# Local and global attention feeding a gated MLP on one core: a second block of two token tiles, and eight more steps turned on TensorE

## Chip, core and metric

The kernel runs on one core of a Trainium2 chip. The metric is the device time of one execution in microseconds (us). Engines are named as in the profile: PE is TensorE's matmul, PEld its weight load, DVE is VectorE, ACT is ScalarE, POOL is GpSimd, SP is SyncE, which here only issues DMAs. L580 is line 580 of the kernel.

## What is computed

For 8 batches and 8 heads of 64, 512 local and 32 global tokens: a local query sees the 32 global keys and the local keys no more than 32 positions away; a global query sees all keys. The result (4352 tokens of 512) goes through a two-layer MLP with 2048 hidden features.

```python
s_g = scale * np.matmul(q_g, k_all.transpose(0, 1, 3, 2))
out_g = np.matmul(sm(s_g), v_all)
s_ll = np.where(mask, scale * np.matmul(q_l, k_l.transpose(0, 1, 3, 2)), -1000000000.0)
s_lg = scale * np.matmul(q_l, k_g.transpose(0, 1, 3, 2))
out_l = np.matmul(sm(np.concatenate([s_lg, s_ll], axis=-1)), np.concatenate([v_g, v_l], axis=2))
x = out of attention, heads side by side
h = x @ w_in
return (h * (1.0 / (1.0 + np.exp(-h))) @ w_out).astype(np.float32)
```

## The kernel before

**Tokens and blocks.** The 4352 tokens are 34 tiles of 128: 32 local ones (batch and quarter of its 512 positions) and two of global tokens, tile 16 and tile 33. `SIZES` groups the tiles into 12 blocks: ten of three tiles and two of two at the end. For each block the MLP runs over 16 slices f of the hidden features. `first_layer` (L580) makes h for the block's tokens with 12 matmuls of 384 columns (256 in a block of two): each product is split into xh·wh, xl·wh, xh·wl. ACT takes a tanh (L586), DVE multiplies (L587), ACT rounds to gh (L589), DVE takes the remainder gl (L590). `second_layer` (L602 to L604) adds gh·wh, gh·wl, gl·wh into a PSUM bank per tile, three matmuls of 512 columns for each tile. On PE the second layer of slice f stands behind the first layer of slice f+1.

**Attention steps.** A local tile's attention is four steps k, one for each pair of heads, so steps 4t to 4t+3 belong to local tile t (of the first 16; k counts from 0, so the title's words "13 to 20" are k = 12 to 19). A step has parts:
- `st_load` (L310, L312) and, once for a tile, `st_vload` (L322): DMAs on SP's queue; from k = 28 on `st_split` (L332 to L334) makes rounded values and remainders. Steps under 28 score in fp32 (L348), the later ones in two passes (L350, L351).
- `st_scores`: scores on PE, mask and row minimum on DVE (L355), exponentials on ACT (L359), two small operations on DVE (L361, L362), the scaling of one head on ACT (L363) and one on DVE (L364). The result is a tile of probabilities.
- The probabilities must be turned, since the next matmul contracts over keys. A step under `KF` = 12 does it in `st_turn` with four transposes on PE (L392) into a PSUM bank and one copy by ACT into the tile pt (L394). A step from `KF` on uses DRAM: `st_halves` (L374) parts the fp32 words into 16-bit halves with two POOL copies, `st_away` (L379) writes them to DRAM by DMA, `st_back` (L383) brings them back with a transposing DMA. In both cases POOL adds the columns of the global queries to pt (L401, and L404 for a batch's last tile).
- `st_out` (L425): once for a tile, all four steps' outputs on PE; ACT and DVE write the MLP's inputs xh and xl (L432, L433) and DVE adds up the global part (L439).

There are four pt tiles, so a step's pt is free again when the outputs of the tile before are done. Global queries have their own parts (`g_load` L229, `g_scores` L256 to L262, `g_soft` L276 to L281, `g_turn` L296 to L302).

**Order.** PE's order is written out by hand. Every part gets a due time in units of one step (`DUE`; for steps from `KF` on also `DMAT`), the parts are sorted by it, and `fill` advances through this list after each first layer and after each tile's second layer. While block n runs, the list is advanced from the end mark of block n's tiles to that of block n+1's:

```python
            advance(ends[n] + (ends[n + 1] - ends[n]) * min(1.0, now[1] / total / FULL))
```

So a block carries the attention steps of the next block's tiles. With the turn on PE a step's turn is due 1.6 units after its scores and the outputs 2.2; with the way through DRAM the halves are due at 0.7, the DMA away at 1.05, the DMA back at 1.65 and the outputs at 2.7.

**Weights.** While block 0 runs the 16 weight blocks still arrive: SP fetches them (L193), ACT and DVE join their 64-bit words to fp32 (L209, L211, L212), ACT rounds (L221, w_hi) and DVE takes the remainder (L222, w_lo), one block ahead of the slice that uses it. The other engines' orders come from the framework's scheduler, except that operations wrapped in `hold` keep the program's order.

## Time and profile before

| what | value |
|---|---|
| three runs | 991.98, 995.24, 998.11 us (median 995.24) |
| the profiled execution | 994.48 us, span 992.6 us |
| first L580 matmul of block 0 | 47.5 us after the span's start |
| first L580 matmul of block 1 | 150.0 us |
| first L580 matmul of the blocks of two tiles | 891.8 and 940.5 us |
| DMA queue of SP | 148.6 MB, 55.3% of 16 engines' time |
| granted TensorE clock | 0.999 of full speed |

How it is read: matmuls are pipelined and their modelled spans overlap, so the busy time of PE is more than what it needs. The weight loads, one ahead of each matmul, are the better measure of its progress. A wait is put down to the releaser that came last by the profile. In a row of a group stand the line, engine, operation, tiles, shapes and count, then the busy time and the mean ns of one, then the idle time ahead of it and what ended it. In a row of a stretch stand its limits and length, then busy us and count of PE, PEld, DVE, ACT and POOL, the granted clock, the DMA engines' share and GB/s. A row of the timeline has start and length in us first.

### The profile page before, as it was taken

The page shows a single profiled execution, that of the slowest core. Times are in us where ns is not written, and L with a number is a line of the kernel's source. Part 1 is how long each engine was busy: PE and PEld are TensorE (multiplying, and loading weights), DVE is VectorE, ACT ScalarE, POOL GpSimd, SP SyncE. Part 2 cuts the span into 40 slices and gives each one's busy share as a digit, 9 for nine tenths or more (in the row PEclk, how much of TensorE's full clock was granted, in tenths as well). Part 3 has the DMA queues.
Part 4 walks back from the last instruction along what each step waited for, and adds up shares of the span by engine and source line. Part 5 has one row for each costly group of instructions (what it writes and reads, how often), then busy time and mean ns, then how long its engine had stood idle before and what let it go on. Part 6 is the DMA issues. An engine that isn't in the chain of part 4 may idle for free.

```text
span 992.6 us, 17536 instructions
## 1 busy us (share of the span) xinstructions
PE 962.2 (97%) x5790; PEld 846.9 (85%) x5790; DVE 627.6 (63%) x1894; ACT 574.4 (58%) x1479; POOL 200.8 (20%) x413
## 2 busy tenths in 40 slices
PE   8989899999999999999999999999999999999997
PEld 6667678899898889998899989998988999889896
DVE  4889975666676667745577566766667665453322
ACT  7977764556566656644566556666556655343332
POOL 2112221222122212111222222222122221220000
PEclk9999999999999999999999999999999999999999
DMA  8699967566665666534655666566665664433000
GB/s 287 224 289 262 236 169 195 154 169 168 168 168 130 197 178 164 161 98 128 170 151 160 154 178 177 165 183 154 173 175 156 155 164 141 116 91 86 1 22 22
DMA packets 190026, 157.33 MB, mean 159 GB/s; under 512 B 128752, under 2 KB 148720, under 8 KB 189936
## 3 DMA queue, kind: packets, MB, share of 16 engines
q1 hardware_dynamic: 185712, 148.61, 55.3%
q10 hardware_dynamic: 4224, 7.60, 2.2%
q8 instruction: 46, 0.75, 0.3%
q14 instruction: 44, 0.36, 0.1%
HBM read 86.44 MB, written 39.32 MB: 127 GB/s over the span
## 4 chain that ended last, share of the span: by engine, by line
PE 72%; DMA 9%; DVE 4%; ACT 3%; issue 2%; SPq 1%; POOL 0%; ACTq 0%; DVEq 0%; POOLq 0%
PE h L580 29%; PE out L602 10%; PE out L604 10%; PE out L603 10%; PE o L425 6%; DMA raw<-in_qk_dram 5%; DMA raw_g<-in_gqk_dram 2%; PE s L350 2%; PE s L351 2%; DMA away<-halves 1%; ACT qk L332 1%; DVE w L212 1%; DVE gl L590 1%; PE gt L296 1%; DVE w_lo L222 0%
## 5 line engine op out<-in xcount | busy, mean ns | idle before, releaser
L374 POOL COPY halves<-probs 128x512 uint16<-128x512 uint16 x232 | 154.1, 686 | 529.3 <-issue 319.7
L580 PE MATMUL h<-xh,w_lo 128*128 128x384 f32 (+1 forms) x768 | 252.9, 329 | 6.8 <-DVE w_lo L222 6.7
L580 PE MATMUL h<-xh,w_hi 128*128 128x384 f32 (+1 forms) x768 | 252.6, 329 | 0.4 <-ACT w_hi L221 0.3
L580 PE MATMUL h<-xl,w_hi 128*128 128x384 f32 (+1 forms) x768 | 251.5, 327 | 0.0
L602 PE MATMUL out<-w_hi,gh 128*128 128x512 f32 x544 | 221.2, 407 | 6.2 <-ACT gh L589 6.2
L604 PE MATMUL out<-w_hi,gl 128*128 128x512 f32 x544 | 215.6, 396 | 3.6 <-DVE gl L590 3.2
L603 PE MATMUL out<-w_lo,gh 128*128 128x512 f32 x544 | 213.9, 393 | 0.0
L586 ACT ACTIVATE t<-h 128x384 f32<-128x384 f32 (+1 forms) x192 | 90.4, 471 | 176.3 <-PE h L580 162.6
L587 DVE SCALAR_TENSOR_TENSOR t<-t,h 128x384 f32<-128x384 f32 (+1 forms) x192 | 101.7, 530 | 103.5 <-ACT t L586 102.5
L580 PEld LDWEIGHTS h<-xh,w_lo 128*128 128x128 f32 x768 | 144.4, 188 | 9.7 <-DVE w_lo L222 9.7
L580 PEld LDWEIGHTS h<-xh,w_hi 128*128 128x128 f32 x768 | 144.6, 188 | 8.6 <-ACT w_hi L221 1.2
L359 ACT ACTIVATE probs<-probs,st 128x224 f32<-128x224 f32 x244 | 115.7, 475 | 61.7 <-DVE st L355 60.7
L580 PEld LDWEIGHTS h<-xl,w_hi 128*128 128x128 f32 x768 | 144.6, 188 | 6.7 <-DVE xl L433 0.2
L590 DVE TENSOR_TENSOR gl<-t,gh 128x384 fp32r<-128x384 f32 (+1 forms) x192 | 106.2, 553 | 61.5 <-PE out L604 51.3
L604 PEld LDWEIGHTS out<-w_hi,gl 128*128 128x128 f32 x544 | 102.1, 188 | 33.8 <-DVE gl L590 11.0
L589 ACT CAST gh<-t 128x384 fp32r<-128x384 f32 (+1 forms) x192 | 94.3, 491 | 58.2 <-DVE t L587 58.0
L602 PEld LDWEIGHTS out<-w_hi,gh 128*128 128x128 f32 x544 | 102.6, 189 | 28.1 <-ACT gh L589 11.6
L355 DVE CUSTOM_DVE_ANT_0 probs<-s,mask 128x224 f32<-128x224 f32 x244 | 85.7, 387 | 60.0 <-PE s L351 51.1
L603 PEld LDWEIGHTS out<-w_lo,gh 128*128 128x128 f32 x544 | 102.7, 189 | 12.7
L332 ACT CAST qk<-raw 128x704 fp32r<-128x704 f32 x100 | 77.7, 777 | 40.3 <-DMA raw<-in_qk_dram 35.2
L333 DVE TENSOR_TENSOR klo<-raw,qk 128x448 fp32r<-128x448 f32 x100 | 67.0, 670 | 44.5 <-ACT qk L332 43.0
L363 ACT ACTIVATE probs<-probs,st 128x224 f32<-128x224 f32 x122 | 58.7, 481 | 39.4 <-DVE st L362 35.0
(91 smaller groups left out, 1063.0 us busy)
## 6 DMA issues: line engine op xcount, KB each, us to landing
raw<-in_qk_dram SPq DMA_DIRECT2D x100, 352.0 KB, 3.5
away<-halves SPq DMA_DIRECT2D x116, 256.0 KB, 2.6
vraw<-in_v_dram SPq DMA_DIRECT2D x30, 512.0 KB, 5.0
raw_w<-in_wts_dram SPq DMA_DIRECT2D x24, 512.0 KB, 5.9
raw_g<-in_gqk_dram SPq DMA_DIRECT2D x32, 304.0 KB, 4.4
out_dram<-o ACTq DMA_DIRECT2D x28, 256.0 KB, 3.7
raw<-in_qk_dram SPq DMA_DIRECT2D x28, 240.0 KB, 4.1
raw_w<-in_wts_dram SPq DMA_DIRECT2D x16, 256.0 KB, 4.4
```

The lines of the kernel that those rows point to most:

```text
L332: nc.scalar.copy(out=qk, in_=raw)
L355: nc.vector.tensor_tensor_reduce(out=p[:, u, :W], in0=ss[u], in1=mask_of[c], scale=-SCALE, scalar=3.0e38, op0=ALU.add, op1=ALU.min, accum_ ...
L359: nc.scalar.activation(p[:, u, :W], p[:, u, :W], AF.Exp, bias=st[:, u : u + 1], scale=-1.0, accum_out=st[:, 2 + u : 3 + u])
L374: nc.gpsimd.tensor_copy(out=halves[:, :, u], in_=p[:, 2 * P * u : 2 * P * (u + 1)].bitcast(U16).rearrange("p (j h) -> p h j", h=2))
L580: nc.tensor.matmul(h[:, :nt], wt, x[:, c, :nt], start=(i == 0), stop=(i == 3 * NCC - 1))
L586: nc.scalar.activation(t[:, :nt], h[:, :nt], AF.Tanh, scale=0.5)
L587: nc.vector.scalar_tensor_tensor(out=t[:, :nt], in0=t[:, :nt], scalar=1.0, in1=h[:, :nt], op0=ALU.add, op1=ALU.mult)
L589: nc.scalar.copy(out=gh[:, :nt], in_=t[:, :nt])
L590: nc.vector.tensor_tensor(out=gl[:, :nt], in0=t[:, :nt], in1=gh[:, :nt].bitcast(F32), op=ALU.subtract)
L602: nc.tensor.matmul(o, gh[:, sl], wh, start=(f == 0), stop=False)
L603: nc.tensor.matmul(o, gh[:, sl], wl, start=False, stop=False)
L604: nc.tensor.matmul(o, gl[:, sl], wh, start=False, stop=(f == NF - 1))
```

## The change

Two constants:

```diff
-SIZES = (3,) * 10 + (2, 2)
+SIZES = (3, 2) + (3,) * 9 + (2,)
...
-KF = 12
+KF = 20
```

The number of blocks (12) and the numbers of blocks of three and of two stay. Block 1 has two tiles and block 10, the last but one, three. Block 0 so carries steps 12 to 19 and not 12 to 23, and block 1 carries steps 20 to 31. Steps 12 to 19 take the branch of `st_turn` that has transposes; their halves, away and back are gone, and their due times are those of `DUE`:

```python
        due = dict(DUE)
        if k >= KF:
            due.update(DMAT)
            due.update({} if pr else DMAT0)
```

**SP in block 0.** Here the queue before, for two steps (raw is a step's queries and keys, raw_w a weight block, half of it from 0 and 1):

```order
L310 DMA raw_802<-in_qk_dram 128x480
L379 DMA away_810<-halves_793 128x1024
L193 DMA raw_w_839<-in_wts_dram 128x1024
L193 DMA raw_w_841<-in_wts_dram 128x1024
L383 DMA_TRANSPOSE pt_130<-away_810 128x4x256
L310 DMA raw_873<-in_qk_dram 128x480
L379 DMA away_897<-halves_875 128x1024
L193 DMA raw_w_906<-in_wts_dram 128x1024
L193 DMA raw_w_0_908<-in_wts_dram 128x512
L193 DMA raw_w_1_909<-in_wts_dram 128x512
L383 DMA_TRANSPOSE pt_131<-away_897 128x4x256
```

And in the changed kernel, from the load that stands at the same weight block:

```order
L193 DMA raw_w_818<-in_wts_dram 128x1024
L193 DMA raw_w_820<-in_wts_dram 128x1024
L310 DMA raw_863<-in_qk_dram 128x480
L193 DMA raw_w_886<-in_wts_dram 128x1024
L193 DMA raw_w_0_888<-in_wts_dram 128x512
L193 DMA raw_w_1_889<-in_wts_dram 128x512
L193 DMA raw_w_940<-in_wts_dram 128x1024
L310 DMA raw_975<-in_qk_dram 128x480
```

The DMAs away and back are gone from between the weight fetches, and a step's load comes about once in two weight blocks.

**ACT in block 0.** Before, from the tanh of slice 10 to that of slice 11 (gh is what PE's second layer of slice 10 waits for):

```order
L586 ACTIVATE t_10_1468<-h_10_1455 128x384
L363 ACTIVATE probs_86<-probs_86,st_1422 128x224
L209 ACTIVATE w_1433<-raw_w_1230 128x512
L209 ACTIVATE w_1433<-raw_w_0_1301 128x256
L209 ACTIVATE w_1433<-raw_w_1_1302 128x256
L221 CAST w_hi_1449<-w_1361 128x512 x2
L589 CAST gh_10_1469<-t_10_1468 128x384
```

And now, from the same tanh:

```order
L586 ACTIVATE t_10_1400<-h_10_1387 128x384
L363 ACTIVATE probs_85<-probs_85,st_1350 128x224
L209 ACTIVATE w_1365<-raw_w_1129 128x512
L209 ACTIVATE w_1365<-raw_w_0_1216 128x256
L209 ACTIVATE w_1365<-raw_w_1_1217 128x256
L221 CAST w_hi_1381<-w_1298 128x512 x2
L394 COPY pt_130<-t_1412 128x4x128
L209 ACTIVATE w_1425<-raw_w_1214 128x512
L209 ACTIVATE w_1425<-raw_w_0_1310 128x256
L209 ACTIVATE w_1425<-raw_w_1_1311 128x256
L589 CAST gh_10_1401<-t_10_1400 128x384
```

The PSUM copy of a turned step and a second weight's join stand ahead of gh in this slice; in other slices gh comes first, as it did.

**PE in block 1.** Now, from the fourth scores of local tile 5 (step 23) to the outputs of that tile; left out are only rows of the two MLP layers, and the outputs' middle rows:

```order
L348 MATMUL s_1800<-raw_1703 128x224 x2
...
L256 MATMUL gs_2_0_1849<-raw_g_0_1755 64x272
L256 MATMUL gs_2_0_1852<-raw_g_0_1755 64x272
...
L348 MATMUL s_1864<-raw_1768 128x224 x2
...
L348 MATMUL s_1910<-raw_1844 128x224 x2
...
L425 MATMUL o_1946<-pt_129,vraw_1739 64x160 x2
...
L425 MATMUL o_1955<-pt_132,vraw_1739 64x128 x2
```

Between the first row and the outputs stand three second layers and three first layers of two tiles each, two further scores and one global head. In block 1 before, the same stretch had layers of three tiles.

## Prediction

> **What bounds the kernel now.** I read the page first (busy shares, then the chain that ended last), then TensorE's waits in the first block, then the busy times block by block, then VectorE's and ScalarE's rows of the blocks that the change touches. The page's first part and its chain:

> ```profile
> PE 962.2 (97%) x5790; PEld 846.9 (85%) x5790; DVE 627.6 (63%) x1894; ACT 574.4 (58%) x1479; POOL 200.8 (20%) x413
> ...
> PE 72%; DMA 9%; DVE 4%; ACT 3%; issue 2%; SPq 1%; POOL 0%; ACTq 0%; DVEq 0%; POOLq 0%
> ```

> TensorE (PE) sets the end. Its matmul spans overlap, so 97% hides waits; the weight loads (PEld) show them. Next, the busy times of four stretches (PE, PEld, DVE, ACT, POOL, granted clock, DMA share, GB/s). Their limits are the first L580 matmul of a block and that of the next: block 0, block 1, block 7, block 10 (the first of the two blocks of two tiles).

> ```profile
> 47.50:150.00 102.50, 92.09 (x499) 75.35 (x498) 88.87 (x245) 71.30 (x185) 22.90 (x39) 1.00 0.85 236
> 150.00:236.90 86.90, 85.26 (x503) 74.61 (x502) 53.35 (x164) 49.79 (x131) 19.72 (x40) 1.00 0.62 164
> 649.00:731.00 82.00, 82.00 (x502) 74.28 (x501) 54.53 (x167) 50.02 (x128) 18.34 (x37) 1.00 0.62 167
> 891.80:940.50 48.70, 48.70 (x328) 43.92 (x327) 17.26 (x46) 17.38 (x45) 2.74 (x4) 1.00 0.16 44
> ```

> In blocks 7 and 10 PE never pauses, and PEld is busy 0.906 and 0.902 of the time. I take 0.905 as the share of a PE that waits for nobody. Block 0 then needs 75.35 / 0.905 = 83.3 us and takes 102.5: 19.2 us lost. Block 1 needs 82.4 and takes 86.9: 4.5 lost. Block 0 is the only place with much to win, and in it VectorE (DVE) is busy 87% and the DMA engines 85%. Whom PE waited for there:

> ```profile
> PE h L580 <- DVE w_lo L222: 6.7, 6, 2.1
> PE o L425 <- POOL pt L401: 2.3, 2, 1.3
> PE out L602 <- ACT gh L589: 0.3, 1, 0.3
> ```

> First DVE, which joins and splits a weight block per f besides its share of the attention, then two waits at the attention outputs. Other losses are pieces of 0.1 to 0.7 us.

> **The change part by part.** Two numbers move. The second block has two token tiles, so while block 0 runs the stream must bring only tiles 3 and 4 (8 steps, not 12), and the 12 steps of tiles 5 to 7 fall into block 1, which is a tile narrower. And steps 12 to 19, exactly those of block 0 now, are turned by four transposes on PE and a PSUM copy on ScalarE (ACT), not by POOL halves, a DMA out and a transposing DMA back.

> *Matmul work.* Two blocks of two tiles there were and are, so the MoE matmuls are the same set.

> *Transposes.* PE's weight loads near 37 us, and the PSUM copy on ACT:

> ```profile
> 36.98 0.42 PEld L392 LDWEIGHTS t<-ident,probs 128*128 128x128 f32 x4 [1.03 <-ACT probs L363]
> 37.37 0.68 PEld L348 LDWEIGHTS s<-raw 128*128 128x128 f32 x4
> 38.70 0.47 PEld L425 LDWEIGHTS o<-pt,vraw 128*64 128x64 f32 x8 [0.24 <-issue]
> 39.92 0.65 PEld L256 LDWEIGHTS gs<-raw_g 128*64 128x64 f32 x4 [0.17 <-issue]
> ...
> 34.82 0.56 ACT L394 COPY pt<-t 128x512 f32<-128x512 f32 x1
> ```

> Four transposes cost 0.42 / 0.905 = 0.46 us, eight steps **3.7 us** of PE, and nothing on PE goes away for them. From below 8 x 0.42 = 3.4; from above 8 x 0.66 = 5.3, with the whole matmul span of such a group. In the same way a step's scores in fp32 (L348) cost 0.75, its outputs (L425) 0.52, a global head (L256) 0.72.

> *Block 0.* Four steps and two global heads leave it: PE needs 83.3 - 4 x (0.75 + 0.52) - 2 x 0.72 + 3.7 = 80.5 us. DVE's rows of block 0:

> ```profile
> L355 DVE CUSTOM_DVE_ANT_0 probs<-s,mask 128x224 f32<-128x224 f32 x26 | 9.2, 381 | 1.0 <-PE s L348 1.0
> L364 DVE TENSOR_SCALAR probs<-probs,st 128x224 f32<-128x224 f32 x13 | 4.4, 337 | 0.5
> L433 DVE TENSOR_TENSOR xl<-o,xh 128x256 fp32r<-128x256 f32 (+1 forms) x7 | 2.8, 394 | 0.9 <-ACT xh L432 0.9
> L276 DVE TENSOR_REDUCE gst<-pg 128x1 f32<-128x544 f32 x3 | 2.1, 712 | 1.4 <-ACT pg L257 1.4
> L362 DVE RECIPROCAL st<-st 128x2 f32<-128x2 f32 x13 | 2.1, 164 | 0.4
> L355 DVE DVE_READ_ACCUMULATOR2_ANT st<- 128x1 f32 x26 | 2.1, 80 | 0.0
> L281 DVE TENSOR_SCALAR pg<-pg,gst 128x544 f32<-128x544 f32 x2 | 1.1, 552 | 0.1
> ```

> A step is 2 x (0.381 + 0.080) + 0.337 + 2 x 0.164 = 1.59 us (L361 as L362), four 6.3. One global softmax (0.71 + 0.55 + three of some 0.15) 1.7, two L433 and their accumulations some 1.2. So 9.2 us leave DVE. More goes with the halves copies: DVE and POOL disturb each other. The first L212 below runs while POOL copies halves, the second alone:

> ```profile
> 73.09 1.09 DVE L212 SCALAR_TENSOR_TENSOR w<-w,raw_w 128x512 uint32<-128x512 uint32 x1 [0.48 <-ACT w L209]
> 75.06 0.68 DVE L212 SCALAR_TENSOR_TENSOR w<-w,raw_w 128x512 uint32<-128x512 uint32 x1
> ...
> 132.64 1.10 DVE L212 SCALAR_TENSOR_TENSOR w<-w,raw_w 128x512 uint32<-128x512 uint32 x1 [0.47 <-ACT w L209]
> ...
> 72.40 1.24 POOL L374 COPY halves<-probs 128x512 uint16<-128x512 uint16 x2 [11.81 <-DMA raw_w<-in_wts_dram]
> ```

> That is 0.41 us for a meeting. Ten L212 of block 0 meet a copy (the last at 132.64), and all but a few of the copies leave it: some nine meetings, about 3.6 us. DVE falls from 88.9 to 76 us. [...]

> At DVE's present share (0.867) 76 us is 87.7 us of block 0; by PE alone it is 80.5 and with today's loss untouched 99.7. I take **89 us**, near the DVE figure, because six of the named waits are DVE's and the two L425 waits (2.3 us) lose their cause, but a little above: ACT gets 8 x 0.57 = 4.6 us of copies, which in its new order stand ahead of gh casts that PE's second layer waits for. Loss 8.5 instead of 19.2: **-10.7 us** (bounds -16 and 0). The DMA engines lose 8 x 2 transfers there; the raw tiles and weights come no later.

> *Block 1.* Two tiles: from block 10, (48.7 - 0.5 - 4 x 0.52) / 16 = 2.88 us for one f, 46.1 for sixteen. With 13 scores (some 7 at 0.75, the rest, of fp32r form, at some 0.45), 12 outputs, four heads and the turns of the global rows (some 1) PE needs 46.1 + 8 + 6.2 + 2.9 + 1 = 64 us. The other engines' work is not narrower in proportion:

> ```profile
> L332 ACT CAST qk<-raw 128x704 fp32r<-128x704 f32 x12 | 9.3, 775 | 10.0 <-DMA raw<-in_qk_dram 10.0
> L359 ACT ACTIVATE probs<-probs,st 128x224 f32<-128x224 f32 x26 | 12.3, 474 | 9.3 <-DVE st L355 9.2
> L363 ACT ACTIVATE probs<-probs,st 128x224 f32<-128x224 f32 x12 | 5.8, 482 | 2.4 <-DVE probs L364 1.4 <-DVE st L362 0.5
> ...
> L589 ACT CAST gh<-t 128x256 fp32r<-128x256 f32 (+1 forms) x17 | 7.0, 410 | 6.8 <-DVE t L587 6.8
> L586 ACT ACTIVATE t<-h 128x256 f32<-128x256 f32 x16 | 6.1, 384 | 20.8 <-PE h L580 20.0 <-DVE xl L459 0.8
> ```

> ACT: 13 x (2 x (0.474 + 0.19) + 0.482) + 8 x 0.775 + 16 x (0.410 + 0.384) and some 11 of smaller rows: 53 of 64 us, 83%, against 57% in block 1 now. The second thing that gets short is time. A probability tile must be scored, normalised, halved, sent away and brought back before its outputs; for the fourth step of two tiles:

> ```profile
> 190.80 0.27 PE L351 MATMUL s<-klo,qk 128*128 128x224 f32 x1
> 206.87 2.61 PE L425 MATMUL o<-pt,vraw 128*64 128x160 f32 x32
> ...
> 196.32 0.35 SPq L379 DMA_DIRECT2D away<-halves  x1
> 198.46 1.23 SPq L383 DMA_TRANSPOSE pt<-away  x1
> ...
> 94.99 0.92 PE L348 MATMUL s<-raw 128*128 128x224 f32 x4
> 110.36 1.23 SPq L383 DMA_TRANSPOSE pt<-away  x1
> 116.42 0.71 PE L425 MATMUL o<-pt,vraw 128*64 128x160 f32 x8 [1.29 <-POOL pt L401]
> DMA to landing us min/median/max: 3.0/3.3/7.0
> ```

> In block 1 the scores end at 191.1, the transposing DMA is issued at 198.5 and needs 3.3 us: ready 10.7 us after the scores, used after 15.8. In block 0 it was ready only 20.5 us after (95.9 to 116.4), and PE waited 1.29 us. In the changed order the fourth scores of a tile stand three f, two other scores and one head ahead of the outputs: 3 x 2.88 + 2 x 0.75 + 0.72 = 10.9 us. So the good case just fits and each microsecond of delay on ACT, POOL or the DMA queue is a wait. I take 1.5 us at each of the three outputs and 4.5 us, as now, of small losses: 9 us instead of 4.5, **+4.5 us** (bounds -2 and +16). All of PE is queued behind such a wait, the next first layer too.

> *The rest.* Block 9 gets 12 steps instead of 8 and block 10 a third tile; full blocks lose 1 to 3 us, so **+0.5** (-1 to +2).

> Sum: 3.7 - 10.7 + 4.5 + 0.5 = -2.0 us. The profiled execution took 994.48 us (span 992.6 and 1.9 around it), 0.8 under the median of the three runs (995.24). So **992.5 us**.

> **The rivals.**
> *A, block 1 absorbs its steps.* The small losses stay at 4.5 and the outputs never wait, while DVE, no longer the fullest queue of block 0, lets its loss fall to 4 us. For it: blocks 7 and 10 run without a pause. Against: ACT at 83%, and fp32 steps that are as long on ACT and DVE as ever. 994.5 + 3.7 - 15.2 + 0 = 983.
> *B, slower: the way through DRAM decides in block 1.* One mechanism: SP's queue is served in order, a transposing DMA waits in it for its tile's outward DMA to land, and the next tile's loads and outward DMA stand behind it. If from scores to arrival it takes 17 us, between the two cases above, each of the three outputs waits 17 - 10.9 = 6.1 us, 18 in all, 14 more than I allow: 992.5 + 14 = 1006.5. It decides against the change once the way takes about 15 us.
> *C, block 0 keeps its loss.* The waits for w_lo come from the order of DVE's queue (a join of 2 us ahead of a split), not its load, and the new copies on ACT hold gh back. Loss 16 instead of 19.2: 994.5 + 3.7 - 3.2 + 4.5 + 0.5 = 1000. For it: the joins and splits are the same number and still stand in pairs.
> *D, the change moves nothing but names* can't be: 8 pairs of DMAs are gone from SP's order.

> **How the numbers follow.** Forecast 0.47 (985 to 999 by its own), A 0.20, B 0.13, C 0.20. A measurement of this kernel tells about 1% from no change (its three runs spread over 6 us). Faster by over 1% is below 985.3: nearly all of A and a little of the forecast, 0.21; slower by over 1% is above 1005.2: most of B and a tail of C, 0.13; the rest 0.66. The range goes from 983 to 1005, to A's middle and short of B's.

> **What would show it.** In the changed profile block 0 (first L580 to the first of 256 columns) should last 87 to 92 us, with DVE busy about 76 us, no wait of L425 for POOL, and six waits for w_lo shrunk to under 4 us. Block 1 should last 70 to 76 us with ACT above 70%, and PE's waits there should name gh, gl and pt (L401, or the DMA itself). Later blocks should keep their lengths. It is wrong if block 0 stays above 96 us (C), if block 1 takes under 68 (A) or above 84 (B).

## The result, and the profile after

The changed kernel takes 1006.39 us (median of four runs, 1005.91 to 1011.55) against 994.63 for the kernel before: a ratio of 1.0129, with a 95% interval of 1.0107 to 1.0151. It is slower by 11.8 us, where 2 us less were forecast. The profiled execution has a span of 1004.2 us, 11.6 more than before.

First the busy times of the first four blocks of the changed kernel (limits and length, then busy us and count of PE, PEld, DVE, ACT and POOL, the granted clock, the DMA engines' share, GB/s):

```profile
47.40:146.90 99.50, 89.46 (x476) 75.69 (x475) 77.55 (x211) 67.98 (x167) 4.83 (x12) 0.97 0.53 169
146.90:226.30 79.40, 71.45 (x466) 60.53 (x465) 44.62 (x157) 43.64 (x128) 19.44 (x40) 0.96 0.65 165
226.30:308.30 82.00, 80.66 (x490) 72.59 (x489) 55.00 (x170) 50.08 (x126) 20.11 (x40) 1.00 0.65 173
308.30:396.60 88.30, 84.37 (x499) 74.94 (x498) 54.66 (x166) 49.69 (x128) 18.28 (x37) 0.98 0.59 156
```

Block 0 has its lighter load (DVE 77.6 us instead of 88.9, POOL 4.8 instead of 22.9, DMA 53% instead of 85%) and yet takes 99.5 us. Block 1 takes 79.4, and block 3, which the change hardly touches, 88.3. The clock column has changed too: before, all four rows read 1.00.

Whom PE waited for, in the whole run:

```profile
PE s L350 <- DVE qk L334: 6.7, 3, 3.4
PE h L580 <- DVE w_lo L222: 6.1, 6, 2.1
PE out L602 <- ACT gh L589: 4.2, 3, 2.3
PE out L604 <- DVE gl L590: 3.6, 5, 1.1
...
PE o L425 <- issue: 0.4, 1, 0.4
```

The waits for w_lo are where they were (6.7 before, now 6.1). The outputs (L425) no longer wait for POOL. New is the first row: scores that wait for L334, the last part of `st_split`. It stands in block 1. Its first case is step 28, seen on SP, ACT, DVE and PE:

```profile
171.83 0.50 SPq L379 DMA_DIRECT2D away<-halves  x1
172.43 0.38 SPq L229 DMA_DIRECT2D raw_g<-in_gqk_dram  x1
176.54 1.47 SPq L383 DMA_TRANSPOSE pt<-away  x1
178.11 0.53 SPq L312 DMA_DIRECT2D raw<-in_qk_dram  x1
...
182.06 0.78 ACT L332 CAST qk<-raw 128x704 fp32r<-128x704 f32 x1 [3.10 <-DMA raw<-in_qk_dram]
...
182.87 0.63 DVE L333 TENSOR_TENSOR klo<-raw,qk 128x448 fp32r<-128x448 f32 x1 [3.46 <-ACT qk L332]
183.51 0.42 DVE L334 TENSOR_TENSOR qk<-raw,qk 64x256 fp32r<-64x256 f32 x1
...
184.08 0.34 PE L350 MATMUL s<-qk 128*128 128x224 f32 x1 [1.82 <-DVE qk L334]
```

SP's queue sits from 172.8 to 176.5 in front of L383, which waits for its DMA away to land. Only behind it the raw tile is asked for, at 178.1, and it is in use at 182.1. ACT stands still for 3.10 us, DVE for 3.46, and PE for 1.82. For step 29, from the view of the chain that ended last (start and length in us; rows of 0.05 us and less left out):

```profile
178.69 3.98 DMA away<-halves
...
182.68 1.23 SPq L383
...
184.03 4.26 DMA raw<-in_qk_dram
...
188.32 0.79 ACT qk L332
...
189.13 0.63 DVE klo L333
...
189.77 0.74 DVE qk L334
```

Each link waits for the one above it, and PE's scores of step 29 wait 1.53 us for the last. In all of block 1, ACT's waits for raw tiles are:

```profile
ACT qk L332 <- DMA raw<-in_qk_dram: 10.0, 5, 3.1
```

The second new thing, in PE's rows near one of the old waits (the profile's own record of the clock has 0.5 from 89.95 to 93.37):

```profile
87.17 0.33 PE L580 MATMUL h<-xh,w_hi 128*128 128x384 f32 x1
87.34 0.33 PE L580 MATMUL h<-xl,w_hi 128*128 128x384 f32 x1
89.75 0.53 PE L580 MATMUL h<-xh,w_lo 128*128 128x384 f32 x1 [2.08 <-DVE w_lo L222]
90.08 0.52 PE L580 MATMUL h<-xh,w_hi 128*128 128x384 f32 x1
90.40 0.52 PE L580 MATMUL h<-xl,w_hi 128*128 128x384 f32 x1
```

After the wait a matmul of 384 columns starts every 0.32 us; ahead of it, every 0.17. The clock is halved. In the changed kernel's trace there are five such stretches of 3.41 us each before the end (two in block 0, two in block 1, one in block 3), in that of the kernel before none. In all five some matmul is in flight throughout, so I count each at half its length, 1.7 us, and all five at some 8.5 us. That is an estimate; no run has the same waits without the half speed.

### The profile page after: what moved, and what is told of

Same layout as the page of the kernel before. It is cut to its first block, busy times and chain, and to the rows that moved or that the text cites. A ratio compares the mean times of both kernels' runs of the same rounds, so it can differ in the third digit from the quotient of the medians.

```text
span 1004.2 us, 17544 instructions
## 1 busy us (share of the span) xinstructions
PE 970.2 (97%) x5822; PEld 857.6 (85%) x5822; DVE 620.2 (62%) x1894; ACT 578.6 (58%) x1487; POOL 183.8 (18%) x397
## 4 chain that ended last, share of the span: by engine, by line
PE 83%; DVE 6%; DMA 5%; ACT 4%; issue 1%; SPq 1%; ACTq 0%; DVEq 0%
PE h L580 33%; PE out L602 11%; PE out L604 11%; PE out L603 11%; PE o L425 6%; DMA raw<-in_qk_dram 3%; PE s L350 2%; PE s L351 2%; PE s L348 1%; DMA away<-halves 1%; DVE w L212 1%; PE gs L256 1%; ACT w L209 1%; ACT probs L359 1%; PE gt L296 1%
## 5 line engine op out<-in xcount | busy, mean ns | idle before, releaser
L580 PE MATMUL h<-xh,w_lo 128*128 128x384 f32 (+1 forms) x768 | 253.9, 331 | 6.1 <-DVE w_lo L222 6.1
L580 PE MATMUL h<-xh,w_hi 128*128 128x384 f32 (+1 forms) x768 | 255.1, 332 | 0.8 <-ACT w_hi L221 0.7
L580 PE MATMUL h<-xl,w_hi 128*128 128x384 f32 (+1 forms) x768 | 252.7, 329 | 0.0
L374 POOL COPY halves<-probs 128x512 uint16<-128x512 uint16 x216 | 138.7, 664 | 476.5 <-issue 287.0
L602 PE MATMUL out<-w_hi,gh 128*128 128x512 f32 x544 | 221.4, 407 | 4.2 <-ACT gh L589 4.2
L586 ACT ACTIVATE t<-h 128x384 f32<-128x384 f32 (+1 forms) x192 | 90.5, 472 | 187.7 <-PE h L580 174.0
L587 DVE SCALAR_TENSOR_TENSOR t<-t,h 128x384 f32<-128x384 f32 (+1 forms) x192 | 101.7, 530 | 118.0 <-ACT t L586 116.9
L580 PEld LDWEIGHTS h<-xh,w_hi 128*128 128x128 f32 x768 | 146.1, 190 | 9.2 <-ACT w_hi L221 1.5
L580 PEld LDWEIGHTS h<-xh,w_lo 128*128 128x128 f32 x768 | 145.7, 190 | 8.0 <-DVE w_lo L222 8.0
L580 PEld LDWEIGHTS h<-xl,w_hi 128*128 128x128 f32 x768 | 146.0, 190 | 6.5
L359 ACT ACTIVATE probs<-probs,st 128x224 f32<-128x224 f32 x244 | 115.7, 475 | 60.3 <-DVE st L355 59.6
L589 ACT CAST gh<-t 128x384 fp32r<-128x384 f32 (+1 forms) x192 | 94.3, 491 | 53.0 <-DVE t L587 52.7
L602 PEld LDWEIGHTS out<-w_hi,gh 128*128 128x128 f32 x544 | 103.1, 189 | 24.2 <-ACT gh L589 7.0
L355 DVE CUSTOM_DVE_ANT_0 probs<-s,mask 128x224 f32<-128x224 f32 x244 | 85.5, 388 | 52.5 <-PE s L351 44.3
L332 ACT CAST qk<-raw 128x704 fp32r<-128x704 f32 x100 | 77.7, 777 | 39.7 <-DMA raw<-in_qk_dram 37.5
L333 DVE TENSOR_TENSOR klo<-raw,qk 128x448 fp32r<-128x448 f32 x100 | 67.3, 673 | 44.9 <-ACT qk L332 43.6
L363 ACT ACTIVATE probs<-probs,st 128x224 f32<-128x224 f32 x122 | 58.7, 481 | 42.7 <-DVE st L362 40.2
```

The source lines that it names most:

```text
L332: nc.scalar.copy(out=qk, in_=raw)
L355: nc.vector.tensor_tensor_reduce(out=p[:, u, :W], in0=ss[u], in1=mask_of[c], scale=-SCALE, scalar=3.0e38, op0=ALU.add, op1=ALU.min, accum_ ...
L359: nc.scalar.activation(p[:, u, :W], p[:, u, :W], AF.Exp, bias=st[:, u : u + 1], scale=-1.0, accum_out=st[:, 2 + u : 3 + u])
L374: nc.gpsimd.tensor_copy(out=halves[:, :, u], in_=p[:, 2 * P * u : 2 * P * (u + 1)].bitcast(U16).rearrange("p (j h) -> p h j", h=2))
L580: nc.tensor.matmul(h[:, :nt], wt, x[:, c, :nt], start=(i == 0), stop=(i == 3 * NCC - 1))
L586: nc.scalar.activation(t[:, :nt], h[:, :nt], AF.Tanh, scale=0.5)
```

## The experiments

The theory (A in the expectations): the narrow second block makes the raw tiles late through SP's queue; block 0 waits because of the order on DVE and ACT and not their load; and pauses of PE bring the half-speed stretches. Rivals: the transposes and PSUM copies cost the time; ACT and DVE are simply full; the half-speed stretches have another cause. Lengths of the first blocks in us, from first L580 to first L580, the half-speed stretches before the end, and the medians of all runs. They come from four sessions, in which the kernel before took 994.6 (first two rows), 994.0 (next four), 995.8 (next three) and 997.0 us (last two):

| kernel | block 0 | block 1 | block 2 | block 3 | half-speed stretches of 3.41 us | total |
|---|---|---|---|---|---|---|
| before | 102.5 | 87.0 | 86.1 | 82.6 | 0 | 994.6 |
| changed | 99.5 | 79.4 | 82.0 | 88.3 | 5 | 1006.4 |
| sizes only | 98.7 | 79.3 | 81.3 | 88.1 | 5 | 1005.0 |
| turns only | 105.8 | 87.3 | 85.7 | 82.2 | 1 | 994.8 |
| changed, load first | 99.3 | 71.8 | 80.1 | 81.6 | 2 | 988.7 |
| changed, split earlier | 86.7 | 81.1 | 83.1 | 88.8 | 6 | 995.5 |
| changed, both mends | 85.2 | 71.7 | 80.1 | 81.8 | 0 | 976.8 |
| before, load first | 102.5 | 84.0 | 82.9 | 81.0 | 0 | 985.1 |
| before, both mends | 98.9 | 84.0 | 82.5 | 80.8 | 2 | 980.9 |
| sizes only, both mends | 89.3 | 73.5 | 80.1 | 81.8 | 3 | 980.9 |
| turns only, both mends | 99.7 | 84.0 | 82.5 | 81.1 | 1 | 981.6 |

**The halves of the change.** The sizes alone:

```diff
-KF = 20
+KF = 12
```

> Only the block sizes of the change (second block of two tiles); steps 12 to 19 go through DRAM as before. Theory A (the narrow second block is what costs: SP's queue brings the raw tiles too late for the splits, PE waits for DVE L334, and pauses bring half-speed clock windows): block 1 lasts 76 to 82 us as in the changed kernel (79.4, against a need of 64), PE waits for L334 again by 4 to 9 us, total 1000 to 1007. Rival B (the transposes and the PSUM copies on ACT are what costs): block 1 under 72 us, total 990 to 996.

Measured 1005.03 us, ratio 1.0121 (1.0089 to 1.0152). Block 1 lasts 79.3 us and waits in the same place, even longer:

```profile
PE s L350 <- DVE qk L334: 9.1, 4, 3.1
```

The turns alone (the kernel before, with the limit moved):

```diff
-KF = 12
+KF = 20
```

> Only the turns of the change: steps 12 to 19 on TensorE, block sizes as before. Theory A: block 1 of three tiles keeps its 87 us, no wait for L334 over 1 us there; block 0 gets 3.7 us of transposes and loses the two L425 waits (2.3) and some DVE time, 98 to 104 us; total 991 to 998. Rival B: block 0 gets longer than 106 us, total 1001 to 1007.

994.80 us, ratio 1.0012 (0.9999 to 1.0025). Block 0 is longer than expected (105.8, not 98 to 104), though under the rival's 106, and the total is that of before. So the sizes make the kernel slower, and the turns are not the cause.

**SP's queue.** The changed kernel, with the transposing DMA due later, which puts the next load ahead of it:

```diff
-DMAT = dict(load=-1.65, halves=0.7, away=1.05, turn=1.3, back=1.65, out=2.7)
+DMAT = dict(load=-1.65, halves=0.7, away=1.05, turn=1.3, back=2.0, out=2.7)
```

> The changed kernel with one swap in SP's queue: the transposing DMA is due at 2.0 instead of 1.65, so that a step's raw load stands ahead of it and no longer behind its wait for the DMA away. Theory A: the waits of PE for L334 in block 1 fall from 6.7 us to under 3, block 1 from 79.4 to 69 to 75 us, total 997 to 1002. Rival (the waits for L334 come from ACT and DVE being full in the narrow block, the load is not what is late): they stay above 5 us and the total at 1004 to 1008. If the later DMA back makes the outputs wait, L425 shows waits of over 3 us and the total stays as well.

988.67 us, ratio 0.9948 (0.9933 to 0.9963): 17.7 us under the changed kernel, more than expected, and faster than the kernel before. Block 1's row, SP's queue near step 28, and PE's waits in block 1:

```profile
147.20:219.00 71.80, 67.62 (x466) 58.01 (x465) 43.79 (x153) 43.87 (x128) 19.44 (x40) 1.00 0.70 186
```

```profile
174.26 0.38 SPq L229 DMA_DIRECT2D raw_g<-in_gqk_dram  x1
177.97 0.33 SPq L312 DMA_DIRECT2D raw<-in_qk_dram  x1
178.59 1.69 SPq L383 DMA_TRANSPOSE pt<-away  x1
180.34 0.57 SPq L379 DMA_DIRECT2D away<-halves  x1
181.82 0.33 SPq L312 DMA_DIRECT2D raw<-in_qk_dram  x1
183.54 1.23 SPq L383 DMA_TRANSPOSE pt<-away  x1
```

```profile
PE o L425 <- DMA pt<-away: 2.4, 2, 1.6
PE s L350 <- DVE qk L334: 1.7, 1, 1.7
```

And ACT's waits for raw tiles there:

```profile
ACT qk L332 <- DMA raw<-in_qk_dram: 2.1, 3, 1.3
```

Both raw loads now stand ahead of L383. Step 28's goes out at 178.0, hardly earlier than before, but for another reason: it waits 3.3 us for its buffer, until PE has finished the scores of step 27 at 177.95. In the changed kernel that buffer was free at 176.1, and the load still went out at 178.1. PE no longer waits at the scores of steps 28 and 29. The same ACT and DVE work (43.9 and 43.8 us busy) fits into 71.8 us; those engines were not too full. The waits for L334 fall from 6.7 to 1.7, ACT's for raw tiles from 10.0 to 2.1, and the later DMA back costs 2.4 at the outputs. Block 3 loses its excess too: in the changed kernel ACT waited there for raw tiles (9.0 us in four waits), and behind such a wait, and a shorter one for DVE, a gh cast came 2.3 us late for PE. Here ACT waits 1.4 us for raw tiles, PE has no listed wait, and the block lasts 81.6 us.

**The order of the weight split.** The changed kernel, one slice more ahead:

```diff
-            while len(w_hi) < NF and len(w_hi) <= NF * n + f + 1:
+            while len(w_hi) < NF and len(w_hi) <= NF * n + f + 2:
```

> The changed kernel with the split of a weight block into w_hi and w_lo one slice earlier in ACT's and DVE's order; the same work. Theory A (block 0 waits because of the order of DVE's queue, not its load, 78%): PE's waits for w_lo in block 0 fall from 6.1 us to under 2, block 0 from 99.5 to 90 to 95 us, total 996 to 1002. Rival (DVE and ACT have no more to give, the wait only moves): block 0 stays at 97 to 101 us with longer waits for gh and gl, total 1004 to 1008.

995.50 us, ratio 1.0004 (0.9984 to 1.0025): 10.9 us under the changed kernel. Block 0's row, and PE's only listed wait in it:

```profile
47.30:134.00 86.70, 84.95 (x476) 74.93 (x475) 75.61 (x211) 68.81 (x168) 5.86 (x12) 0.98 0.60 192
```

```profile
PE out L602 <- ACT gh L589: 1.8, 1, 1.8
```

The same work of DVE and ACT, started one slice earlier, takes 12.8 us off block 0, more than the theory asked for. All waits for w_lo are gone, and the rest of the kernel stays about as it was (block 1 81.1, block 3 88.8).

**Both, on the changed kernel and on the kernel before.**

> The changed kernel with both mends: the load ahead of the transposing DMA in SP's queue, and the weight split one slice earlier. Theory A (the two losses are separate: block 0 by the order on DVE and ACT, blocks 1 to 3 by SP's queue): the gains add, block 0 85 to 89 us, block 1 69 to 73, total 974 to 981. Rival (one loss only hands the time to the other): 984 to 990.

976.76 us, ratio 0.9796 (0.9764 to 0.9829). The gains add, to about 1 us: 1006.4 - 17.7 - 10.9 = 977.8. No stretch at half speed is left before the end.

> The kernel before (block sizes 3 x 10, 2, 2 and the turn on TensorE under step 12) with the same two mends. Theory A: block 0 falls from 102.5 to 91 to 97 us and the later blocks lose some small waits; total 978 to 986. Compared with the changed kernel under the same mends it tells what the change is worth once SP's queue is not late: theory A expects the two within 1% of each other, the rival (a narrow second block is bad in itself) expects the kernel before to be ahead by 8 us or more.

980.88 us, ratio 0.9846 (0.9811 to 0.9880). The total is as expected; block 0 is not (98.9 us): with the way through DRAM still in it, PE waits 4.9 us for raw tiles, and has two half-speed stretches. The changed kernel is ahead by 4.1 us on the same chip in the same session (975.26 to 977.88 against 980.38 to 984.15).

> The kernel before with the load ahead of the transposing DMA alone. Theory A: SP's queue has slack in blocks of three tiles, so the swap brings little here: 988 to 994. Rival (the swap helps anywhere by about as much as in the changed kernel, 17 us): 975 to 980.

985.06 us, ratio 0.9882 (0.9845 to 0.9920): better than I expected of slack blocks. Blocks 1 to 3 of the kernel before give up 3.0, 3.2 and 1.6 us. In the whole run PE's waits for gh and gl, which ACT's casts feed, fall from 9.4 to 2.7 us. So SP's queue was probably late there as well, only less; this is argued and not shown, since ACT's waits for raw tiles in block 1 fall only from 10.0 to 8.3.

**The half speed.** The kernel before with chains of tiny matmuls ahead of five first layers in blocks 4 to 9, each link waiting for an ACT copy:

```diff
+    def pause(bank, n):
+        for _ in range(n):
+            hold(nc.tensor.matmul(bank[:32, 3 * P : 3 * P + 32], idle, idle, start=True, stop=True))
+            hold(nc.scalar.copy(out=idle[:32], in_=bank[:32, 3 * P : 3 * P + 32]))
...
+        pause(h, PAUSES.get((n, f), 0))
...
+PAUSES = {(4, 6): 2, (4, 12): 3, (6, 6): 4, (7, 6): 6, (9, 6): 8}
```

> The kernel before with five pauses put on TensorE where it otherwise never waits: chains of 2, 3, 4, 6 and 8 tiny matmuls, each waiting for an ACT copy of the one before (about 0.7 us a link, so pauses of some 0.7, 1.4, 2.1, 3.5 and 4.9 us). Theory A (a pause that leaves TensorE idle for half of one 3.41 us window brings a next window at half clock): half-speed windows right behind the two or three longest pauses, none behind the two shortest, each costing some 1.7 us beyond the pause; total 1004 to 1014. Rival (the half-speed windows of the changed kernel come from something else, as the load on the chip): no half-speed window at the pauses, 1003 to 1008.

1024.59 us (two runs), more than either side expected, for two reasons. ACT was often late for a chain's first copy: the chain of four cost 5.1 us and not 2.1, its first wait alone 3.56 (a later link took some 0.51). And blocks 0 to 2, which have no chains, got four half-speed stretches and are together 7.5 us longer than in the kernel before. The prediction on the clock held. Behind the chains of four, six and eight there are two half-speed stretches each, behind those of two and three none, and none elsewhere in blocks 4 to 9; the granted clock of the whole execution is 0.982. The chain of four, cut into stretches that follow the clock's own steps:

```profile
606.80:610.30 3.50, 2.83 (x16) 2.23 (x14) 1.67 (x4) 2.36 (x4) 1.07 (x2) 1.00 0.84 268
610.30:613.70 3.40, 0.19 (x1) 0.09 (x1) 2.46 (x11) 1.78 (x8) 0.71 (x2) 1.00 0.68 194
613.70:617.10 3.40, 2.76 (x9) 2.56 (x10) 0.00 (x0) 0.35 (x2) 0.47 (x1) 0.55 0.95 244
617.10:620.50 3.40, 3.40 (x11) 3.01 (x11) 0.55 (x1) 0.90 (x2) 0.00 (x0) 0.50 0.40 77
```

In the second row PE is all but idle at full clock; in the two after it the clock is halved, the second time although PE was busy 81% of the time in the stretch before. So here a pause (3.56 us, and 0.32 three times behind it) was enough to bring the half speed. That every half-speed stretch of the changed kernel has this cause is inferred from their place behind its waits.

**Which part of the change is worth something under the mends.** The sizes without the turns, and the turns without the sizes:

> The changed block sizes with both mends, but the turn of steps 12 to 19 through DRAM (step 12 as the limit). Theory A (sizes and turns matter little by themselves, the order matters): 974 to 981. If the turns on TensorE carry the gain of the mended kernel: 982 or more, with L425 or L348 waiting for DMAs in block 0.

> The block sizes before with both mends and steps 12 to 19 turned on TensorE. In the kernel before with both mends block 0 still lasts 98.9 us and PE waits there for a raw tile (4.9 us). If those waits come from the DMAs away and back in SP's queue, block 0 falls to 90 to 95 us and the total to 974 to 979; if they come from the weight fetches, it stays at 979 to 984.

980.85 us (ratio 0.9830, 0.9796 to 0.9864) and 981.61 us (0.9840, 0.9803 to 0.9878): the first at the upper end of theory A's range, the second in the range of the weight fetches. Without the turns PE waits for DMAs back at the outputs (L425, 4.8 us, 3.8 of it in block 0). Without the sizes block 0 stays at 99.7 us, and PE waits there 2.7 us for raw tiles and 2.5 for a global one, so those waits are not due to the DMAs away and back alone; that the weight fetches cause them is not shown. Both medians lie 4 to 5 us above that of the whole change with the mends, but that one is of another session and chip and the intervals of the ratios overlap. So it is not shown that the two halves need each other.

## Why the prediction was wrong

The forecast was 992.5 us and the likeliest sign a small gain; the kernel is slower. Of the 13.6 us between the forecast change (-2.0) and that of the profiled executions (+11.6), block 0's term is off by 10.5 and block 1's by 6.4, and the rest is 3.3 better than forecast. Point by point, with the terms as they stood:

- **Transposes, +3.7.** About right. In the changed kernel's block 0 the 32 weight loads of L392 are busy 4.3 us, against the 3.4 that eight times 0.42 makes, partly at half speed.
- **Block 0, -10.7.** This step failed. PE's need was about right (80.5; in the changed kernel with both mends, where nothing runs at half speed, block 0's weight loads of 74.05 us make 81.8), and so was DVE's load (76 us forecast, 77.6 measured), but against that need the loss went from 19.2 to 19.0 and not to 8.5. I took the length from DVE's share of busy time. The waits for w_lo came from where the split stood in the queues, close ahead of its use: with 11 us less on DVE they changed by 0.6 us, and with the split one slice earlier they went. That was rival C, to which I gave 0.20. The run with the turns alone says the same: block 0 is 3.3 us longer, and PE's waits for w_lo are 6.7 us as before.
- **Block 1, +4.5.** The mechanism was half right and mis-sized: 15.4 us were lost against a need of 64, so +10.9. I named SP's in-order queue (rival B), but let it hit the outputs, whose way I had measured. The outputs did not wait. What was late was the raw tile that stands behind L383 in the same queue, and from step 28 on it has ACT, then DVE twice, between it and PE. The row of L332 that I quoted for its duration ends with "10.0 <-DMA raw<-in_qk_dram": in block 1 of the kernel before, ACT already waited 10 us for raw tiles, and PE did not wait for L334 there; presumably the wider layers covered it. I read the busy half of that row and not the idle half.
- **ACT in block 1, 53 of 64 us.** Wrong as well: it was busy 43.6 us, 55% of the block, and the sign "above 70%" failed. I added up the durations of rows, but they overlap: of the changed kernel's 128 ACT instructions in block 1 they add up to 51.6 us, and the cast of L332 at 182.06 lasts 0.78 us while the next instruction starts at 182.74. So ACT was late for its tiles and not full, as the run with the load ahead of L383 showed.
- **The rest, +0.5.** It came to some -2.8 (11.6 less the three terms above), although block 3 alone lost 5.7 us more; block 2 (4.1 us shorter) and block 5 (2.9 shorter) gained more than that.
- **What was in no step: the clock.** I read a granted clock of 1.00 as a constant. Five half-speed stretches, by my estimate some 8.5 us of the 11.6, lie inside the losses of blocks 0, 1 and 3. I priced a PE wait at its length, and those of about 2 us that took up half of the 3.41 us ahead of a half-speed stretch (2.08 at 87.7, 1.82 at 182.3) cost, by the same estimate, 1.7 us more. The time of rival B (1006.5) came out by luck, with a different bill.

## What to carry to other kernels

In a queue that sits in front of a wait, as SP's did from 172.8 to 176.5, find for every wait what is queued behind it and where that goes next; an engine's "idle, released by DMA" at no cost today (ACT's 10.0 us in block 1 before) can be the first bill when the block around it gets shorter. A busy share says what an engine could do, not when it does the one thing that is waited for: move that thing one iteration earlier before taking work away. And look at the granted clock behind a TensorE pause: behind pauses of 1.82 and 2.08 us it was 0.5 here for 3.41 us, which belongs to their price.

## What the runs showed of the hardware

So a pause need not fill a piece: 2.08 us at 87.7 sufficed, while waits of up to 2.1 us in block 0 of the kernel before did nothing. Cut in pieces of the same length, back from the point where its clock falls behind the last matmul (991.18), the lowest piece of that block is at 0.62, that of the whole trace from block 0 on at 0.57. The kernel with the chains, the same as the kernel before up to block 3, had four such stretches in blocks 0 to 2. The four runs of the changed kernel have granted clocks of 0.989 to 0.993, so they are no chance of one execution. The kernel before is not free of them either: its 36 executions beside the experiments have 0.990 to 1.000, all but two of them above 0.993.
